# A decode step's attention: TensorE's middle steps as a loop with its own semaphores, and V in loads of 64 KB a partition

## The chip, the cores and the metric

The kernel runs on one core of one Trainium2 chip. The metric is the device time of one execution in microseconds (us): the median of the runs shown is 2523.11 us, the three lie between 2523.05 and 2523.18.

The engines named below are TensorE (PE, matrix products), VectorE (DVE), ScalarE (ACT), GpSimd (POOL) and SyncE (SP), which here issues the loads. They synchronise through semaphores. SBUF is the on-chip memory of 128 partitions, PSUM the accumulators that TensorE writes. HBM, the memory that holds the inputs, is read by 16 DMA engines.

## The reference: what is computed

One token is decoded. A gate mixes an attention over a cache of 65536 positions in 32 heads with a small feed-forward network:

```python
q = (x @ wq).reshape(B, Sq, H, Dh) ...            # H = 32 heads, Dh = 128
scores = jnp.einsum("bhqd,bhkd->bhqk", q, k_cache) * (Dh ** -0.5)   # 65536 keys a head
p = _softmax(scores, axis=-1)
o = jnp.einsum("bhqk,bhkd->bhqd", p, v_cache)
a = o... @ wo                                      # [32*128] @ [4096, 512]
b = (_silu(x @ w_gate) * (x @ w_up)) @ w_down      # 512 -> 1792 -> 512
g = _sigmoid((x * gate_w).sum(-1, keepdims=True))
out = g * a + (1 - g) * b
```

All inputs are bf16. The two caches are 512 MiB each and are read once; everything else together is some 14 MB.

## The kernel before

**Tiles.** A head's 65536 positions are cut into four tiles of 16384 positions; a tile is 128 partitions of 128 positions of 128 elements (4 MiB, 32 KB a partition). There are N = 128 tiles and M = 64 pairs of tiles. A pair's 256 positions of a partition lie one behind the other in HBM, so that a pair is one run of 64 KB a partition. SBUF holds three buffers of 64 KB a partition: two slots for K pairs, taken in turn (`take`, `give`), and one buffer for a V pair, `V_buf`.

**Scores.** VectorE multiplies a K tile by the query, which is repeated on all partitions (line 261), and adds the halves of each row in place, 128 to 64 to 32 to 16 elements (line 265). TensorE adds the 16 that are left by products with a unit matrix, four columns at a time (line 274, `scores`), and VectorE sums the last four (line 289, `fold`).

**Softmax.** After a head's four tiles VectorE takes the maximum of each partition (line 295); ScalarE spreads it on a diagonal (line 297), TensorE turns it to all partitions (line 299), VectorE takes the maximum of it (line 304), and ScalarE computes the exponentials of all four tiles at once with their sums (line 308). TensorE adds the sums over the partitions (line 316, `total`).

**Values.** For a V tile TensorE does 32 products (line 330, `values`): four columns of exponentials are the weights, 512 elements of V the moving operand. The result for a head, 4 x 512 in PSUM with the wanted parts in a diagonal of blocks, is gathered by VectorE (lines 350 and 361, `head_copy`), turned by TensorE (line 367, `head_turn`) and scaled by ScalarE into the column `oT` (line 397). At the end the 32 columns are multiplied by `wo` (line 406).

**The order of the work** is written out by hand: each engine does its instructions in the order in which the program lists them, and the waits follow from what each instruction reads and writes. The main loop (line 424) is unrolled over the K pairs i; a head is two steps, `first` and the other. The values of the pair i - 2 are done in step i. SyncE issues all large loads from one queue (line 114). In a `first` step the V buffer is reloaded in two halves, each as soon as the 32 products on that half are done (lines 442 and 451); in the other step the buffer gets one load of the pair after both tiles' products (line 453). After that, in either kind of step, follows the load of the K pair two steps on, once the scores of the pair that held the slot are done. Scores read the K slot itself.

```python
            values(2 * i - 4)
            if first:
                load_v(2 * i - 2)
```

The first two heads' steps also hold the queries (line 158), the gate and the feed-forward network, whose weights are loaded into the buffer of V. The last tiles are loaded in smaller pieces into the buffers that come free, with the two parts of `wo`.

Of the kernel before, what the change touches and what calls it, by code (L numbers as in the profile page):

```python
# [11 lines left out]
P = 128  # L12

NB = 128
PAIR = 2 * NB
SLOTS = 2

QUAD = 4  # L20
# [5 lines left out]
V_CUTS = {3: (0, 64, NB), 2: (0, 64, NB), 1: (0, 32, 64, 96, 112, NB - TURNED, NB)}  # L26
EARLY = 16
LATE_CUTS = (EARLY, 24, 28, 30, 32)

GROUPED = 28  # L30


@with_exitstack
def kernel(
# [28 lines left out]
    assert Dh == P and G == 4 and NBH == 512 and H * D <= PAIR * Dh  # L63
    scale = float(Dh) ** -0.5

    consts = ctx.enter_context(tc.tile_pool(name="consts", bufs=1))
    ring = ctx.enter_context(tc.tile_pool(name="ring", bufs=1))
    small = ctx.enter_context(tc.tile_pool(name="small", bufs=2))
    psum_s = ctx.enter_context(tc.tile_pool(name="psum_s", bufs=2, space=bass.MemoryType.PSUM))
    psum_o = ctx.enter_context(tc.tile_pool(name="psum_o", bufs=2, space=bass.MemoryType.PSUM))  # L70
    psum_a = ctx.enter_context(tc.tile_pool(name="psum_a", bufs=1, space=bass.MemoryType.PSUM))
    psum_m = ctx.enter_context(tc.tile_pool(name="psum_m", bufs=2, space=bass.MemoryType.PSUM))

    ctx.enter_context(tc.manual_schedule())


    free = list(range(SLOTS))
    held = {}

    def take(name):  # L80
        slot = free.pop(0)
        held[name] = slot
        return ring.tile(
            [P, PAIR * Dh], bf16, name=name.split(".")[0], tag=f"slot{slot}"
        )

    def give(name):
        free.append(held.pop(name))


# [3 lines left out]
    consts.tile([P, 96], bf16, name="fill")  # L94
    xT = consts.tile([P, KT], bf16, name="xT")
    gwT = consts.tile([P, KT], bf16, name="gwT")
    with nc.allow_non_contiguous_dma(reason="small"):
        nc.scalar.dma_start(out=xT, in_=A_x[0, 0, :].rearrange("(p t) -> p t", t=KT))
        nc.scalar.dma_start(out=gwT, in_=gate_w.rearrange("(p t) -> p t", t=KT))

    nc.sync.dma_start(  # L101
        out=V_buf[:, : KT * H * Dh], in_=A_wq.rearrange("(p t) f -> p (t f)", t=KT)
    )
    wq_sb = V_buf[:, : KT * H * Dh].rearrange("p (t f) -> p t f", t=KT)

    K_tiles, V_tiles, S_tiles, F_tiles, P_tiles, O_tiles, q_tiles = {}, {}, {}, {}, {}, {}, {}


    def load(view, cache, m, cuts, start=0):
        h, g = divmod(m, MH)  # L110
        rows = cache[0, h, g * PAIR * P : (g + 1) * PAIR * P, :]
        src = rows.rearrange("(p j) d -> p j d", j=PAIR)
        for a, b in zip(cuts[:-1], cuts[1:]):
            nc.sync.dma_start(out=view[:, a:b, :], in_=src[:, start + a : start + b, :])

    def load_k(m):
        view = take(f"K_t.{m}").rearrange("p (j d) -> p j d", d=Dh)
        load(view, A_k_cache, m, (0, NB, PAIR) if m in (0, M - 1) else (0, PAIR))
        for i in range(2):
            K_tiles[2 * m + i] = view[:, i * NB : (i + 1) * NB, :]  # L120

    def load_v(n, half=0, spare=None):
        if n % G == 0 and spare is None:
            view = V_buf.rearrange("p (j d) -> p j d", d=Dh)
            V_tiles[n], V_tiles[n + 1] = view[:, :NB, :], view[:, NB:, :]
            load(view, A_v_cache, n // 2, (0, PAIR))
        else:
            view = V_buf if spare is None else spare
            view = view[:, half * NB * Dh : (half + 1) * NB * Dh]
            V_tiles[n] = view = view.rearrange("p (j d) -> p j d", d=Dh)  # L130
            load(view, A_v_cache, n // 2, V_CUTS.get(N - n, (0, NB)), n % 2 * NB)

    load_k(0)
    load_k(1)

    ident_f = consts.tile([P, P], f32, name="ident_f")
    make_identity(nc, ident_f[:])
    ident_b = consts.tile([P, P], bf16, name="ident_b")
    nc.scalar.activation(out=ident_b, in_=ident_f, func=ACT.Copy)
    ones_f = consts.tile([P, P], f32, name="ones_f")  # L140
    nc.vector.memset(ones_f, 1.0)

    ones_b = consts.tile([P, P], bf16, name="ones_b")
    nc.vector.memset(ones_b, 1.0)

    qT = consts.tile([P, H], f32, name="qT")
    rowsum = consts.tile([P, H], f32, name="rowsum")
    oT = consts.tile([P, H], bf16, name="oT")
    gval = consts.tile([P, 1], f32, name="gval")
    rg = consts.tile([P, H], f32, name="rg")  # L150
    HD = D // 2
    a_ps = [psum_a.tile([1, HD], f32, name=f"a{i}_ps") for i in range(2)]

    def queries():
        q_ps = psum_m.tile([P, H], f32, name="q_ps", tag="misc")
        for h in range(H):
            for t in range(KT):
                nc.tensor.matmul(
                    q_ps[:, h : h + 1],
                    lhsT=wq_sb[:, t, h * Dh : (h + 1) * Dh],  # L160
                    rhs=xT[:, t : t + 1],
# [398 lines left out]
```

## Time and profile before

| | |
|---|---|
| median of the runs shown | 2523.11 us |
| the profiled execution, its own time | 2523.22 us |
| its span, first to last instruction | 2521.4 us |
| TensorE busy / weight loads | 1274.2 us (51%) / 490.8 us |
| VectorE busy | 2260.4 us (90%) |
| ScalarE busy | 100.5 us (4%) |
| moved by DMA | 1088.42 MB, mean 432 GB/s |
| TensorE's mean granted clock | 0.731 of full speed |

The span is cut into 40 slices, and the rows of digits give the busy tenths of each slice for an engine or for the 16 DMA engines together. The chain goes back from the last instruction, at each step to what released it. In the timeline a row holds the start, the duration, the engine, the line of the kernel and the operation with its operands; instructions that follow one another are merged (x64), and the brackets give the idle time just before and what ended it. SPq rows are issues of loads by SyncE, not the transfers themselves.

### The profile page before, as it was taken

The page shows a single profiled execution, that of the slowest core. Times are in us where ns is not written, and L with a number is a line of the kernel's source. Part 1 is how long each engine was busy: PE and PEld are TensorE (multiplying, and loading weights), DVE is VectorE, ACT ScalarE, POOL GpSimd, SP SyncE. Part 2 cuts the span into 40 slices and gives each one's busy share as a digit, 9 for nine tenths or more (in the row PEclk, how much of TensorE's full clock was granted, in tenths as well). Part 3 has the DMA queues.
Part 4 walks back from the last instruction along what each step waited for, and adds up shares of the span by engine and source line. Part 5 has one row for each costly group of instructions (what it writes and reads, how often), then busy time and mean ns, then how long its engine had stood idle before and what let it go on. Part 6 is the DMA issues. An engine that isn't in the chain of part 4 may idle for free.

```text
span 2521.4 us, 12044 instructions
## 1 busy us (share of the span) xinstructions
PE 1274.2 (51%) x5232; PEld 490.8 (19%) x5232; DVE 2260.4 (90%) x830; ACT 100.5 (4%) x317; POOL 0.7 (0%) x6
## 2 busy tenths in 40 slices
PE   3544654536535455444455453554545544446548
PEld 2211211212212122111122121221211211112213
DVE  5899999989999989899999898999998989999993
ACT  0000000000000000000000000000000000000000
POOL 0000000000000000000000000000000000000000
PEclk8767767767767677676777776776767767677779
DMA  9999999999999999999999999999999999999998
GB/s 415 436 434 433 436 435 430 436 434 433 433 430 436 435 432 432 435 433 442 432 433 432 430 435 434 437 432 433 432 436 432 435 437 429 437 432 432 433 432 374
DMA packets 26888, 1088.42 MB, mean 432 GB/s; under 512 B 3154, under 2 KB 3667, under 8 KB 4947
## 3 DMA queue, kind: packets, MB, share of 16 engines
q1 hardware_dynamic: 26546, 1087.65, 99.8%
q8 instruction: 41, 0.67, 0.1%
q14 instruction: 13, 0.10, 0.0%
q10 hardware_dynamic: 288, 0.00, 0.0%
HBM read 1087.64 MB, written 0.00 MB: 431 GB/s over the span
## 4 chain that ended last, share of the span: by engine, by line
DMA 51%; DVE 46%; PE 2%; issue 1%; another core or an unknown queue 0%; DVEq 0%; SPq 0%; ACT 0%
DMA K_t<-in_A_k_cache_dram 49%; DVE K_t L261 23%; DVE K_t L265 20%; PE S_ps L274 2%; DVE o_row L361 1%; DMA V_buf<-in_A_v_cache_dram 1%; DVE S_sb L289 1%; DVE O_sb L350 1%; DMA wo_late<-in_A_wo_dram 1%; PE O_ps L330 0%; DVE top L304 0%; PE a_ps L406 0%; DVEq L261 0%; SPq L101 0%
## 5 line engine op out<-in xcount | busy, mean ns | idle before, releaser
L261 DVE TENSOR_TENSOR K_t<-K_t,q_sb 128x16384 bf16<-128x16384 bf16 x128 | 1111.7, 8685 | 142.8 <-DMA K_t<-in_A_k_cache_dram 142.8
L330 PE MATMUL O_ps<-V_buf,P_sb 128*4 128x512 bf16 x4032 | 986.4, 409 | 361.4 <-DMA V_buf<-in_A_v_cache_dram 360.5
L265 DVE TENSOR_TENSOR K_t<-K_t 128x2048 bf16<-128x2048 bf16 (+1 forms) x372 | 996.0, 2677 | 8.3
L274 PE MATMUL S_ps<-K_t,ident_b 128*128 128x512 bf16 x576 | 208.3, 503 | 807.2 <-DVE K_t L265 806.8
L330 PEld LDWEIGHTS <-P_sb 128*4 128x4 bf16 x4094 | 364.9, 90 | 980.3 <-issue 534.3
L274 PEld LDWEIGHTS <-ident_b 128*128 128x128 bf16 x576 | 62.4, 113 | 899.4 <-issue 877.3
L289 DVE TENSOR_REDUCE S_sb<-S_ps 128x128 f32<-128x512 f32 x128 | 87.4, 683 | 65.9 <-PE S_ps L274 65.9
L397 ACT ACTIVATE oT<-oh_ps,rg 32x1 bf16<-32x1 f32 x112 | 28.6, 255 | 696.9 <-PE oh_ps L367 695.9
L299 PE MATMUL mT_ps<-diag,ones_f 128*128 128x128 f32 x64 | 24.8, 490 | 60.2 <-ACT diag L297 60.1
L173 ACT ACTIVATE q_sb<-qb_ps 128x128 bf16<-128x128 f32 x32 | 8.9, 278 | 911.6 <-PE qb_ps L171 911.6
L299 PEld LDWEIGHTS mT_ps<-diag,ones_f 128*128 128x128 f32 x64 | 15.6, 303 | 88.4 <-ACT diag L297 88.4
L361 DVE TENSOR_REDUCE o_row<-O_sb 4x128 f32<-4x512 f32 x31 | 31.6, 1020 | 1.1
L297 ACT ACTIVATE diag<-ident_f,m 128x128 f32<-128x128 f32 x32 | 12.8, 401 | 353.9 <-DVE m L295 353.9
L527 DVE CAST out_sb<-a_ps 1x256 bf16<-1x256 f32 x1 | 0.4, 412 | 27.2 <-PE a_ps L406 27.2
L308 ACT ACTIVATE P_sb<-S_sb,bias 128x512 bf16<-128x512 f32 x32 | 23.1, 722 | 1.0
L316 PEld LDWEIGHTS tot_ps<-rowsum,ones_f 128*128 128x128 f32 x64 | 20.7, 324 | 12.1 <-issue 9.2
L295 DVE TENSOR_REDUCE m<-S_sb 128x1 f32<-128x512 f32 x32 | 22.0, 686 | 1.1
L350 DVE TENSOR_TENSOR O_sb<-O_ps,ident_f 4x512 f32<-4x512 f32 x31 | 20.8, 671 | 1.5 <-PE O_ps L330 1.5
L306 ACT ACTIVATE bias<-top 128x1 f32<-128x1 f32 x32 | 6.5, 203 | 298.4 <-DVE top L304 298.4
L316 PE MATMUL tot_ps<-rowsum,ones_f 128*128 128x1 f32 x64 | 13.2, 276 | 0.0
L169 ACT ACTIVATE q_diag<-ident_f,qT 128x128 bf16<-128x128 f32 x32 | 12.8, 400 | 0.4
L321 DVE RECIPROCAL recip<-tot_ps 128x1 f32<-128x1 f32 x32 | 5.1, 161 | 7.8 <-PE tot_ps L316 7.8
(53 smaller groups left out, 115.5 us busy)
## 6 DMA issues: line engine op xcount, KB each, us to landing
V_buf<-in_A_v_cache_dram SPq DMA_DIRECT2D x62, 4096.0 KB, 22.5
K_t<-in_A_k_cache_dram SPq DMA_DIRECT2D x4, 4096.0 KB, 31.8
V_buf<-in_A_v_cache_dram SPq DMA_DIRECT2D x4, 2048.0 KB, 21.9
V_buf<-in_A_wq_dram SPq DMA_DIRECT2D x1, 4096.0 KB, 12.4
wo_early<-in_A_v_cache_dram SPq DMA_DIRECT2D x1, 4096.0 KB, 37.0
wo_late<-in_A_v_cache_dram SPq DMA_DIRECT2D x3, 1024.0 KB, 24.1
wo_early<-in_A_wo_dram SPq DMA_DIRECT2D x1, 2048.0 KB
V_buf<-in_B_w_gate_dram SPq DMA_DIRECT2D x1, 1792.0 KB, 54.6
```

The lines of the kernel that those rows point to most:

```text
L261: yield nc.vector.tensor_tensor(out=K, in0=K, in1=q_rep, op=ALU.mult)
L265: yield nc.vector.tensor_tensor(out=K[:, :, 0:half], in0=K[:, :, 0:half], in1=K[:, :, half : 2 * half], op=ALU.add,)
L274: nc.tensor.matmul(S, lhsT=ident_b, rhs=K_tiles[n][:, :, c : c + QUAD], start=(c == 0), stop=(c == width - QUAD),)
L289: nc.vector.tensor_reduce(out=S_tiles[h][:, g * NB : (g + 1) * NB], in_=F_tiles.pop(n), axis=AXIS.X, op=ALU.add)
L295: nc.vector.tensor_reduce(out=m, in_=S_tiles[h], axis=AXIS.X, op=ALU.max)
L299: nc.tensor.matmul(mT_ps, lhsT=ones_f, rhs=diag, start=True, stop=True)
L308: nc.scalar.activation(out=P_tiles[h], in_=S_tiles[h], func=ACT.Exp, bias=bias, scale=scale, accum_out=rowsum[:, h : h + 1],)
L316: nc.tensor.matmul(tot_ps, lhsT=ones_f, rhs=rowsum[:, h : h + 1], start=True, stop=True)
L330: nc.tensor.matmul(O_tiles[h], lhsT=P_tiles[h][:, g * NB + j : g * NB + j + 4], rhs=V_tiles[n][:, j : j + 4, :], start=(g == 0 and j == 0) ...
L350: nc.vector.tensor_tensor(out=O_sb.rearrange("q (c d) -> q c d", c=4), in0=O.rearrange("q (c d) -> q c d", c=4), in1=diag, op=ALU.mult,)
L361: nc.vector.tensor_reduce(out=dst, in_=src, axis=AXIS.X, op=ALU.add)
L397: nc.scalar.activation(out=oT[part * A : (part + 1) * A, g * QUAD + j : g * QUAD + j + 1], in_=oh_ps[j * A : (j + 1) * A, :], func=ACT.Cop ...
```

## The change

The kernel is written anew inside one section in which every wait and every event is explicit; semaphores belong to the kernel and are cleared at its end by GpSimd. The arithmetic on the tiles is the same, in these pieces:

- TensorE's steps 2 to 62 are one loop of 61 rounds with a fixed body (`tensor_step`). Since a count can't grow in a loop's fixed body, TensorE waits for credits: another engine adds one, `take` waits for one and subtracts it.
- Every V pair ahead of the last step is one load of 64 KB a partition (`load_pair`), issued by SyncE when both tiles of the pair before are done (`load_v`); the K load two steps on follows it. GpSimd waits for the V loads and passes each on as a credit (`tell_of_v`).
- All steps have the same order on TensorE: scores of the first tile, a spread of the query, a total, 64 value products, scores of the second tile, a turn of the output, a turn of the maximum.
- VectorE's last add of a tile writes to a small tile of its own, `T_sb`, which the scores read.
- Exponentials, total and output are made per pair, not per head. The output leaves PSUM by ScalarE (`o_copy`), is turned by four products, and the two halves of a head are added by ScalarE (`add_half_o`).
- The last tiles' loads and those of `wo` have a semaphore for each piece.

```diff
-        if i >= 2:
-            values(2 * i - 4)
-            if first:
-                load_v(2 * i - 2)
...
-            values(2 * i - 3)
-            if first:
-                load_v(2 * i - 1, 1)
-            else:
-                load_v(2 * i - 2)
...
+    def load_v(i):
+        wait(sync, pe_V, 2 * i)
+        load_pair(V_buf, A_v_cache, i, v_in)
+
+    def sync_step(m):
+        load_v(m - 1)
+        if m + 2 < M:
+            wait(sync, pe_S, 2 * m + 2)
+            load_k(m + 2)
...
+    def tell_of_v(i):
+        wait(pool, v_in, 16 * (i + 1))
+        pool.sem_inc(c_V, 1)
...
+    def vector_step(m):
+        h, b = divmod(m, MH)
+        width, to = (WIDTH, T_sb) if m < M - 1 else (LAST, None)
+        last = product(2 * m)
+        if b == 0:
+            top_of(h - 1)
+        else:
+            fold(2 * m - 1)
+        add_halves(2 * m, width, last, to)
+        last = product(2 * m + 1)
+        fold(2 * m)
+        if b == 1:
+            weight(h - 1, m - 1)
+        add_halves(2 * m + 1, width, last, to)
+        if b == 1:
+            row_max(h, fold(2 * m + 1))
...
+    def scalar_step(m):
+        h, b = divmod(m, MH)
+        if b == 0:
+            head_bias(h - 1)
+        wait(act, pe_V, 2 * (m - 2))
+        exponentials(h - 1, b, P_sb, PAIR).then_inc(c_P, 1)
+        if m == M - 1:
+            return
+        if b == 1:
+            query(h + 1, True)
+        else:
+            act.sem_inc(c_q, 1)
+        wait(act, pe_V, 2 * (m - 2) + 2)
+        o_copy(h - 1).then_inc(c_o, 1)
+        wait(act, pe_o, m - 1)
+        if b == 0:
+            marks["half_o"] = ac(copy(half_o[:, 0:1], oh))
+            act.sem_inc(c_m, 1)
+        else:
+            ac(head_out(h - 1, add_half_o()))
+            head_diag(h, True)
...
+    def take(credit):
+        pe.wait_ge(credit, 1)
+        pe.sem_inc(credit, -1)
...
+    def tensor_step():
+        take(c_S[0])
+        scores(0, T_sb, WIDTH)
+        take(c_q)
+        query_spread()
+        take(c_P)
+        total()
+        take(c_V)
+        for i in range(2):
+            pe_V(values(P_sb[:, i * NB : (i + 1) * NB], V_half[i], 0, NB, i == 0, i == 1))
+        take(c_S[1])
+        scores(1, T_sb, WIDTH)
+        take(c_o)
+        head_turn()
+        take(c_m)
+        max_turn()
...
+    with tc.tile_critical():
+        prologue()
+        for m in range(2, M):
+            vector_step(m)
+            scalar_step(m)
+            if m < M - 1:
+                sync_step(m)
+            tell_of_v(m - 2)
+        sync_end()
...
+        with pe.Fori(0, M - 3):
+            tensor_step()
+        tensor_end()
+        for engine in (pe, act, dve):
+            engine.sem_inc(done.sem, 1)
+
+        pool.wait_ge(done.sem, 3)
+        pool.wait_ge(out_in.sem, 16)
+        pool.sem_clear(range(first_sem.num, last_sem.num + 1))
```

## The prediction

> **What bounds the kernel now.** I read the page's slices and queues first, then the chain that ended last, then one head's timeline (TensorE, VectorE and SyncE separately), then the waits of SyncE.
>
> ```profile
> DMA  9999999999999999999999999999999999999998
> DMA packets 26888, 1088.42 MB, mean 432 GB/s; under 512 B 3154, under 2 KB 3667, under 8 KB 4947
> q1 hardware_dynamic: 26546, 1087.65, 99.8%
> q8 instruction: 41, 0.67, 0.1%
> ...
> DMA 51%; DVE 46%; PE 2%; issue 1%; another core or an unknown queue 0%; DVEq 0%; SPq 0%; ACT 0%
> ```
>
> The reader is to see that the 16 DMA engines never rest: queue 1 alone fills 99.8% of their span. VectorE is 90% busy and takes nearly half of the chain, but it waits for K in every step, so it follows the DMA. The timeline of one step (K pair to K pair) shows it:
>
> ```profile
> 1236.67 0.33 SPq L114 DMA_DIRECT2D V_buf<-in_A_v_cache_dram  x1
> 1245.62 0.33 SPq L114 DMA_DIRECT2D K_t<-in_A_k_cache_dram  x1
> ...
> 1247.91 8.69 DVE L261 TENSOR_TENSOR K_t<-K_t,q_sb 128x16384 bf16<-128x16384 bf16 x1 [0.87 <-DMA K_t<-in_A_k_cache_dram]
> ...
> 1264.77 1.86 PE L274 MATMUL S_ps<-K_t,ident_b 128*128 128x512 bf16 x4 [16.45 <-DVE K_t L265]
> ...
> 1266.44 0.42 PE L316 MATMUL tot_ps<-rowsum,ones_f 128*128 128x1 f32 x2
> ...
> 1267.16 14.77 PE L330 MATMUL O_ps<-V_buf,P_sb 128*4 128x512 bf16 x64 [0.30 <-DMA V_buf<-in_A_v_cache_dram]
> ...
> 1275.06 7.23 SPq L114 DMA_DIRECT2D V_buf<-in_A_v_cache_dram  x2
> ...
> 1284.59 0.33 SPq L114 DMA_DIRECT2D K_t<-in_A_k_cache_dram  x1
> ...
> 1286.42 8.69 DVE L261 TENSOR_TENSOR K_t<-K_t,q_sb 128x16384 bf16<-128x16384 bf16 x1 [2.67 <-DMA K_t<-in_A_k_cache_dram]
> ```
>
> K lands at 1247.9, the V pair 19.25 us later at 1267.1, the next K at 1286.4. A step is 38.51 us, in which 16 MiB arrive: 435.7 GB/s. The V pair issued at 1236.67 had 11.2 us of K ahead of it in the queue; the next V, in two halves, is issued at 1275.06 and 1281.96 (the row's end less 0.33), again 11.3 us ahead of the landing at 1286.4. That lead is what keeps the queue full, and the change touches it.
>
> I then took all 59 intervals between K landings (starts of the first product of a step that waited for a K load) from 123.93 to 2410.52, 2286.59 us in all, and split them by what V was loaded in them. The 30 with two half loads have a median of 38.745 us, the 29 with one pair load 38.53 us. Two intervals of either kind are some 1.3 us longer, cause unseen.
>
> **The change part by part**, against the profiled execution's own 2523.22 us (span 2521.4, 1.8 around it; the median of the timed runs is 2523.11, so 0.1 less). A measurement here can tell about 0.2%, 5.0 us, from no change.
>
> *The V loads.* 30 pairs of 4 MiB loads become 30 loads of 8 MiB. By the two medians a step with one load is 0.215 us shorter: 30 x 0.215 = 6.4 us off. Ends: nothing, if the difference between the two kinds of step has another cause, and 13.3 us, if every interval came down to 38.53 (2286.59 - 59 x 38.53). I take 6.4, the row of the very operation.
>
> *When the V buffer is refilled.* Before, in every second step, half of it is reloaded after 32 matmuls. Now SyncE waits for all 64 (the V event counts) before any of it, in every step, and the lead falls from 11 us to what is left after 64 matmuls. Queued behind that wait on SyncE is the K load two steps on; behind the K load waits VectorE. The loop is: V landed, the relay through GpSimd, 64 matmuls, issue, landing. The 64 matmuls at one go (29 groups in the middle of the trace) take 14.63 to 15.96 us, mean 15.23; the first few run at a granted clock of 0.5. From their end to the issue it is 0.03 us (the second half above: 1281.93 to 1281.96). From issue to landing on an empty queue the nearest row is the 4096 KB load of the query weights, 12.4 us, where 4 MiB take 9.63 at the rate of the steps: 2.77 us over the bytes, so 19.27 + 2.77 = 22.04 for a pair. The lower end is the output's store, which is issued at 2519.35 while the span ends at 2521.4: at most 2.05 over the bytes, 21.3. Sum: 15.23 + 0.03 + 22.04 = 37.30, against 38.53 for the DMA: 1.23 us to spare, before the relay.
>
> The relay and what else stands ahead of the matmuls: GpSimd's wait and its increment (its queue holds nothing else in these steps), TensorE's wait and decrement (the nearest row is a semaphore hop of 0.06 from ScalarE's diagonal to its matmul), and in program order the scores of the first tile (they start 16.86 us after K landed, 2.4 ahead of V; a step that begins with a fold, 0.68, instead of the maximum, 0.28, starts them 0.4 later), one spread of the query (0.23) and the total (0.42). I put the delay at 0.3 to 1.5 us, part of it at half clock, where a delayed matmul is made up for later; 0.7 as a middle. That leaves 0.5 us a step: the forecast is that V is refilled in time, at no cost. The other end is 15.96 + 1.5 + 22.07 - 38.53 = 1.0 us a step, 61 us over 61 looped steps. Less than nothing it can't be, as the bytes set 38.53.
>
> The Trainium skill (DMA: Bandwidth & Descriptors, Anatomy of one DMA) fits a load as about 2.0 us plus the bytes at 436 GB/s, on GpSimd's path; by it a pair would take 21.2 us instead of 22.04, the spare would be 2.0, and the sum the same. No run shown has an 8 MiB load on an empty queue.
>
> *VectorE.* It loses the two operations that took a head's output out of PSUM (0.67 + 1.02 a head) and gains a sum of two columns (about 0.16, as the other small ones). Its adds now each follow an explicit wait; an event instruction on SyncE has a median of 28 ns, so some 14 of them are 0.4 a step. All of this is hidden: VectorE waits 2.67 and 0.87 us for K in the two steps of a head. Late next is K. If that cover were gone, each us would also push the first scores, and with them the V refill.
>
> *TensorE and ScalarE.* Each step now has a spread, a total of two columns, and a head turn by four float32 products (eight rows of line 380 take 1.02), and ScalarE copies the output (0.59, line 344). TensorE has 16.45 us idle before the first scores of a step, ScalarE is 4% busy: nothing. The second tile's scores move behind all 64 matmuls. VectorE finishes that tile 34.5 us after K landed; the matmuls end at about 19.2 + 0.7 + 15.2 = 35.1; scores 1.03, fold 0.69, maximum 0.69 reach 37.6, ahead of the next K at 38.53. If the matmuls end over 0.9 later, VectorE starts late in every second step, but it has 1.8 a step on average to make that up.
>
> *TensorE's program* is a loop of 61 rounds. Its instruction fetch, 0.67 MB in 41 packets on the same engines, is 1.5 us at 434 GB/s. Ends: 1.5 off and the price in rival 2; I take 1.0 off.
>
> *The start.* The first V reload was issued in halves at 114.50 and 121.41; now it goes at 121.4 whole, landing at 143.4, with the K of 122.75 behind it landing at 162.7, against 162.6 before. Ends 0 and 2.8 (an emptied queue); I take 0.5.
>
> *The end.* GpSimd waits for three engines and the store and clears about 50 semaphores. Nearest: 28 ns each if single, 1.4; or one instruction in place of the present waits of SyncE at the end (0.7 and 0.6), -0.5. I take 0.7. The last loads each get a semaphore of their own and lose their waits (9.0 and 4.1 us on lines 183 and 185), but the queue is never empty there: nothing.
>
> Sum: 2523.2 - 6.4 - 1.0 + 0.5 + 0.7 = 2517.0 us, 0.24% faster.
>
> **The rivals.**
>
> 1. *The refill is late (the other side).* The loop V landed, 64 matmuls, issue, landing becomes longer than 38.53 us and sets the step. It decides where the time from the V landing to the last value matmul passes 16.5 us (38.53 - 22.04). For it: 29 measured groups reach 15.96 without any relay, and with so small a lead an uneven finish of the 16 engines is no longer averaged out. Against it: the mean leaves 1.2 us. At 0.6 us a step it gives 61 x 0.6 = 37 on top of the other terms: 2517 + 37 = 2554. From 0.2 to 1.0 a step: 2529 to 2578.
>
> 2. *The loop's jump costs.* At the jump back TensorE has to get its program again, two packets of 16 KB a round (0.67 MB / 41) or 2 MB in all: 1.3 MB more than before, +3 us, and if a fetch falls among the value matmuls, every us beyond the 0.5 spare is 61 us. For it: the queue for instructions shares the full engines. Against it: the jump stands in a 16 us idle stretch, and a body of some 190 instructions is small. With 0.5 us lost a step: 2517 + 4 + 31 = 2552. The Trainium skill (Runtime: NRT & Kernel Launch, Instruction fetch mechanics) says that a taken branch to a page outside the current two-page window must fetch it before going on; nothing in the profile before shows a branch.
>
> 3. *The merged load gains nothing.* The 0.215 us belong to something else in that step. For it: the four long intervals show that the DMA's pace has causes I don't see. Against it: 21 of the 29 pair steps and 25 of the 30 half steps lie within 0.1 of their own kind's median. Then 2517.0 + 6.4 = 2523.4, no change.
>
> **How the numbers follow.** The refill in time: 0.45; its own range is 2511 (the gain up to 12) to 2521, of which 0.31 lies below 2518.1, the 0.2% line, and 0.14 above. Rival 1: 0.39, of which 0.06 is so small (up to 0.15 us a step) that it ends within 0.2%. Rival 2: 0.08, slower. Rival 3: 0.08, same. So faster 0.31, same 0.28, slower 0.41. The likeliest case gives 2517.0. The range reaches down to 2511 and, for the late refill, up to 2565: some 0.08 of rivals 1 and 2 lies above and 0.04 below.
>
> **What would show it.** Right: intervals between K landings all at 38.53; groups of 64 value matmuls ending within 16.5 us of the V landing; VectorE's idle time still put down to K; few instruction packets. Wrong: intervals well over 38.6 with the DMA share of the slices below 9 tenths or the rate below 430 GB/s, the chain running through value matmuls and V loads (rival 1); TensorE idle among the matmuls of a step with instruction packets beside it (rival 2); alternating intervals gone but none at 38.53 (rival 3). The time is wrong if the lead of 0.5 us is not there: it is the difference of sums near 38 us, and 2% of either decides it.

## The result, and the profile after

The changed kernel takes 2553.6 us (median of four runs, 2552.57 to 2557.16) against 2523.14 us before: a ratio of 1.0122, 95% interval 1.0104 to 1.0139. It is 1.2% slower. The profiled execution took 2553.62 us, with a span of 2551.8 us.

The page of the changed kernel, its slices, queues and chain:

```profile
DMA  9999999999999999999999999999999999999998
DMA packets 22389, 1087.84 MB, mean 426 GB/s; under 512 B 2657, under 2 KB 3170, under 8 KB 4450
...
q1 hardware_dynamic: 22082, 1087.65, 99.1%
q8 instruction: 5, 0.08, 0.0%
...
PE 2%; DVE 0%; ACT 0%; issue 0%
```

The queue of the loads still looks full: every slice but the last reads 9. But its share fell from 99.8% to 99.1%, and the rate from 432 to 426 GB/s with the same bytes. The slices are too coarse for this loss; the rate shows it. The instruction queue went from 41 packets to 5. The chain of this trace covers only the last 2% of the span and says nothing of the steps.

The landing of each K pair is the start of VectorE's first product in a step that waited for a K load. Cut at these landings, the two spans compare like this:

| stretch | before | after | difference | the prediction had |
|---|---|---|---|---|
| start, up to the landing at 162.64 / 167.76 | 162.6 | 167.8 | +5.1 | +0.5 |
| the next 58 steps | 2247.9 | 2267.1 | +19.2 | -7.4 |
| last K landing (2410.52 / 2434.83) to the end | 110.9 | 117.0 | +6.1 | +0.7 |
| span | 2521.4 | 2551.8 | +30.4 | -6.2 |

A step went from 38.76 us on average to 39.09. The loss isn't spread evenly. These are rows of the timeline of the changed kernel, two steps in a row (SyncE's issues of V, VectorE's first product of each step, the value products; the brackets hold the idle time before and what ended it):

```profile
1067.25 0.33 SPq L174 DMA_DIRECT2D V_buf<-in_A_v_cache_dram  x1
1069.98 8.69 DVE L254 TENSOR_TENSOR K_buf<-K_buf,q_sb 128x16384 bf16<-128x16384 bf16 x1 [4.93 <-DMA K_buf<-in_A_k_cache_dram]
1091.51 16.53 PE L457 MATMUL O_ps<-V_buf,P_sb 128*4 128x512 bf16 x64 [1.88 <-PEq L432]
1108.08 0.33 SPq L174 DMA_DIRECT2D V_buf<-in_A_v_cache_dram  x1
1110.92 8.69 DVE L254 TENSOR_TENSOR K_buf<-K_buf,q_sb 128x16384 bf16<-128x16384 bf16 x1 [0.41 <-DMA K_buf<-in_A_k_cache_dram]
1130.40 15.87 PE L457 MATMUL O_ps<-V_buf,P_sb 128*4 128x512 bf16 x64 [0.22 <-PEq L432]
1146.30 0.33 SPq L174 DMA_DIRECT2D V_buf<-in_A_v_cache_dram  x1
1149.58 8.69 DVE L254 TENSOR_TENSOR K_buf<-K_buf,q_sb 128x16384 bf16<-128x16384 bf16 x1 [4.72 <-DMA K_buf<-in_A_k_cache_dram]
```

The V pair issued at 1067.25, 2.73 us ahead of the K landing at 1069.98, lets its products start 24.26 us after the issue; TensorE stood idle for 1.88 us, and the next K landed 40.94 us after the last one. The V pair issued at 1108.08 had much the same lead, 2.84 us, and was on time: products after 22.32 us, a step of 38.66 us.

I call the time from the issue of a V pair to the next K landing its lead. All 56 steps of the changed kernel that the trace shows whole, with the undisturbed steps of this kernel, 38.63 us, as the measure:

| lead of the V load | steps | products start over 20.0 us behind the K landing | mean step, us |
|---|---|---|---|
| 2.4 to 3.1 us | 14 | 6 | 39.63 |
| 3.1 to 3.75 | 22 | 4 | 38.99 |
| 3.75 to 4.25 | 11 | 2 | 38.93 |
| over 4.25 | 9 | 0 | 38.67 |

On time means a start 19.5 us behind the K landing. The 12 late steps hold 19.2 us of the 25.6 us by which these steps exceed 38.63 us each. A late V load makes the K pair behind it late by about as much.

What is late in such a step is a small part of the load. The trace records the landing of each load in sixteen parts, as many as there are DMA engines. Of the V load issued at 1067.25, fourteen parts are in 21.55 to 22.19 us after the issue, the last two after 23.98 and 24.08 us; of the one issued at 1108.08 all sixteen are in after 21.39 to 22.14 us. In each of the 12 late steps the last one to three parts are over 1 us behind the eighth. In the kernel before, the parts of a K load lie even further apart, 4.6 us from first to last (median) and up to 7.5, against 1.5 and 3.5 here, and no step is late: with the longer lead an engine that is ahead has the next load in its queue.

The packets, the pieces in which the DMA engines move a load, show the loss as well. Summed over the 7 us behind each of 58 V issues, a DMA engine of the changed kernel (mean of the sixteen) stands idle for 7.5 us and loses 13.5 us in packets of 64 KB that take longer than their usual 2.42 us. That is 21 us, about the 19.2 us that the steps lost. In the kernel before neither shows: none of its packets of 64 KB in these steps takes over 3 us, 155 of the changed kernel's do.

SyncE's waits in the changed kernel (engine and line, what was waited for: us in total, times, longest) show who holds that load back:

```profile
SPq L174 <- PE O_ps L457: 2291.4, 61, 39.8
SPq L174 <- PE S_ps L436: 97.9, 61, 39.6
```

SyncE waits for the value products in every step; the K load's own condition, the scores behind them, adds about 1 us (97.9 less the one wait of 39.6, over the other 60).

### The profile page after: what moved, and what is told of

Its sections match the earlier page's. It is cut to its first block, busy times and chain, and to the rows that moved or that the text cites. A ratio compares the mean times of both kernels' runs of the same rounds, so it can differ in the third digit from the quotient of the medians.

```text
span 2551.8 us, 13959 instructions
## 1 busy us (share of the span) xinstructions
PE 1344.4 (53%) x5813; PEld 559.9 (22%) x5813; DVE 2217.6 (87%) x802; ACT 187.6 (7%) x503; POOL 0.7 (0%) x6
## 3 DMA queue, kind: packets, MB, share of 16 engines
q1 hardware_dynamic: 22082, 1087.65, 99.1%
## 5 line engine op out<-in xcount | busy, mean ns | idle before, releaser
L254 DVE TENSOR_TENSOR K_buf<-K_buf,q_sb 128x16384 bf16<-128x16384 bf16 x128 | 1112.1, 8688 | 204.3 <-DMA K_buf<-in_A_k_cache_dram 204.3
L265 DVE TENSOR_TENSOR K_buf<-K_buf 128x8192 bf16<-128x8192 bf16 x252 | 849.4, 3371 | 4.3
L436 PE MATMUL S_ps<-T_sb,ident_b 128*128 128x512 bf16 x488 | 180.1, 505 | 1026.4 <-PEq L432 1026.2
L457 PEld LDWEIGHTS O_ps<-V_buf,P_sb 128*4 128x4 bf16 x3968 | 352.6, 90 | 621.7 <-issue 184.6
L436 PEld LDWEIGHTS S_ps<-T_sb,ident_b 128*128 128x128 bf16 x488 | 44.9, 110 | 1115.3 <-issue 1099.0
L323 ACT ACTIVATE O_sb<-O_ps 4x512 f32<-4x512 f32 x63 | 63.5, 1008 | 1306.3 <-PE O_ps L457 1306.3
L265 DVE TENSOR_TENSOR T_sb<-K_buf 128x2048 bf16<-128x2048 bf16 x122 | 149.4, 1224 | 4.2
L465 PE MATMUL oh_ps<-ident_f,O_sb 4*128 4x1 f32 x504 | 64.6, 245 | 10.2 <-PEq L432 9.4
L465 PEld LDWEIGHTS oh_ps<-ident_f,O_sb 4*128 4x128 f32 x504 | 60.7, 186 | 40.0 <-issue 39.5
L453 PEld LDWEIGHTS tot_ps<-rs,ones_f 128*128 128x128 f32 x126 | 34.2, 330 | 18.0 <-issue 17.9
```

Of the source, the lines that this page charges most:

```text
L254: return dv(dve.tensor_tensor(out=K, in0=K, in1=q_rep, op=ALU.mult))
L265: ins = dve.tensor_tensor(out=to, in0=K[:, :, 0:half], in1=K[:, :, half : 2 * half], op=ALU.add)
L323: return act.activation(out=out, in_=in_, func=ACT.Copy, scale=scale)
L436: ins = pe.matmul(S_ps[n % 2], lhsT=ident_b, rhs=src[:, :, c : c + QUAD], start=(c == 0), stop=(c == width - QUAD),)
L453: pe_t(pe.matmul(tot[:, :n], lhsT=ones_f, rhs=rs[:, :n], start=True, stop=True))
L457: ins = pe.matmul(O_ps, lhsT=probs[:, j : j + 4], rhs=view[:, j : j + 4, :], start=(opens and j == start), stop=(closes and j == stop - 4),)
```

## The experiments

The theory to be tested, A: one load of a whole pair can be issued only after all 64 products, some 3.6 us ahead of the K landing instead of 10 to 12, and that is too late. Against it stood: the loop or its jump, the size of the load, and TensorE's half clock in the first products.

### The old kernel with single loads

The kernel before, with every V pair as one load after both tiles' products:

```diff
-            if first:
-                load_v(2 * i - 2)
...
-            if first:
-                load_v(2 * i - 1, 1)
-            else:
-                load_v(2 * i - 2)
+            load_v(2 * i - 2, pair=True)
```

> The kernel before, with one part of the change alone: every V pair is one load of 8 MiB, issued after both tiles' value products; its order on TensorE, its waits and its unrolled program stay. Theory A (the refill comes too late: V landed, 64 products, issue, landing is as long as a step): slower than 2523, since in the steps that are not the first of a head the first tile's scores stand between the two tiles' products, so the issue comes some 1 to 4 us before the next K lands, where it was 11 us; 2545 to 2590. Theory B (the loop, its credits and its relay cost the time, the loads do not): 2517, the 6 us that one load saves over two in 30 steps. Theory C (an 8 MiB V load is itself slower or less even than two of 4 MiB): some 2540, with no relation to the lead.

Measured: 2584.87 us (2569.67 to 2590.97), ratio 1.0252 [1.0234, 1.0269]. In the profiled execution, the fastest of the five, a step takes 39.44 us on average. This part of the change alone, with no loop and no new semaphores, makes the old kernel 2.5% slower. (It is slower than the changed kernel, but it also isn't its order: in every second step the first tile's scores stand between the two tiles' products.) The forecast that V is refilled in time at no cost falls here already.

### The changed kernel with V in halves

```diff
-        wait(sync, pe_V, 2 * i)
-        load_pair(V_buf, A_v_cache, i, v_in)
+        for t in range(2):
+            wait(sync, pe_V, 2 * i - 1 + t)
+            load_tile(V_half[t], A_v_cache, 2 * i + t, v_in)
...
-        wait(pool, v_in, 16 * (i + 1))
+        wait(pool, v_in, 16 * (i + 1) if i == 0 else 32 * i + 16)
```

> The changed kernel, one part undone and more: in every step V is loaded in two halves, each issued when its own tile's 32 products are done; loop, credits and relay stay (the relay waits for both halves). Theory A: the first half is issued some 10 us before the next K lands, the late steps go; steps of 38.75 us (two half loads a step, by the median of such steps before), 61 x (39.09 - 38.75) = 21 us off and some 8 more at the start and the end: 2523 to 2532. Theory B: no change, 2550 to 2557. Theory C: as A.

Measured: 2530.14 us, ratio 1.0026 [1.0016, 1.0036]: 23.5 of the 30.5 us are back. The timeline of one step:

```profile
1235.40 7.24 SPq L178 DMA_DIRECT2D V_buf<-in_A_v_cache_dram  x2
1246.72 8.69 DVE L255 TENSOR_TENSOR K_buf<-K_buf,q_sb 128x16384 bf16<-128x16384 bf16 x1 [1.22 <-DMA K_buf<-in_A_k_cache_dram]
1266.23 15.82 PE L458 MATMUL O_ps<-V_buf,P_sb 128*4 128x512 bf16 x64 [0.25 <-PEq L433]
```

The first half goes out at 1235.40, 11.3 us ahead of the landing; the products start 19.51 us behind it, and take 15.82 us, no less than in the changed kernel. Steps average 38.74 us. The start is back as well: the K pair that landed at 201.17 before lands at 201.38. What remains is the end, 119.1 us from the last K landing (2409.67) to the span's end at 2528.8, against 110.9: TensorE is told only when both halves are there, where the kernel before began on the first half alone. (The next experiment takes 5.0 us of it off.)

### A credit for each half

The same, with a semaphore and a credit for each half:

```diff
+            load_tile(V_half[t], A_v_cache, 2 * i + t, (v_in, vb_in)[t])
...
         pool.sem_inc(c_V, 1)
+        if i:
+            wait(pool, vb_in, 16 * (i))
+        pool.sem_inc(c_V, 1)
...
-        take(c_V)
         for i in range(2):
+            take(c_V)
```

> As the run with V in halves in every step, and TensorE gets a credit for each half and starts on the first as soon as it has landed. Theory A: steps stay at 38.68 (nothing is late any more); at the end, where a chain of TensorE's work runs from the landing of the last pair of V in the looped steps to the last product, that chain starts up to 9 us earlier: 6 to 8 us off 2530, so 2522 to 2524. If the end's loss has another cause: 2530.

Measured: 2524.48 us (2524.11 to 2526.06), ratio 1.0006 [0.9997, 1.0015]. Steps of 38.74 us, 114.1 us behind the last K landing. With V cut in halves and passed on in halves, the loop and the new semaphores are worth the same as the old kernel, as far as can be measured: the loss lies in how V is loaded and passed on.

### The loop written out

```diff
-        with pe.Fori(0, M - 3):
+        for _ in range(M - 3):
             tensor_step()
```

> The changed kernel with TensorE's 61 rounds written out one after the other in place of the loop; credits, order and loads the same. Theory A: no change, 2550 to 2557; the instruction packets return to some 40. Theory B in its form that the jump back costs: 2517 to 2530. Theory C: no change.

Measured: 2563.0 us (2558.75 to 2569.72), ratio 1.0163 [1.0144, 1.0183]. The queues of this kernel's page:

```profile
q8 instruction: 47, 0.77, 0.1%
```

Written out, the kernel is some 9 us slower than with the loop, not equal or faster. Its late steps are as many (12 of 57); its other 45 steps average 38.97 us where those of the loop average 38.77, which by itself is 9 us (the spans of the two profiled executions differ by 7.0 us). So the jump costs nothing that shows, and the rival of the jump falls. That the instruction loads are the reason fits the trace: each of the 42 further packets is 16 KB and takes a DMA engine some 0.9 us, and the 40 steps into which such a packet falls average 39.34 us, the 18 others 38.88 us. No run moved these packets alone.

### More products, a later load

The first value product is done eight more times in each step, 1.75 us at 13.98/64 us a product:

```diff
+        for _ in range(8):
+            pe.matmul(O_ps, lhsT=P_sb[:, 0:4], rhs=V_half[0][:, 0:4, :], start=True, stop=True)
         for i in range(2):
             pe_V(values(...))
```

> The changed kernel with the step's first value product done eight times more ahead of itself (each overwrites, the result is the same): 8 x 0.216 = 1.73 us more from the landing of V to its refill. Theory A: the lead falls by 1 to 1.7 us, and as most steps are already late each gets longer by 0.9 to 1.7 us: 55 to 105 us, 2605 to 2660. Theory C: under 10 us, as TensorE has 16 us idle a step.

Measured: 2648.45 us, ratio 1.051 [1.0489, 1.0531]; the span grew by 86.9 us, 1.42 us in each of 61 steps. In its trace the 72 products take 17.61 us on average, where the 64 took 15.61, so 2.0 us were added, and seven tenths of it reach the end. TensorE is about half idle in the changed kernel (53% busy), and yet most of what is put ahead of the V issue lengthens the step. The circle V landed, products, issue, landing sets the step.

### Half-size loads, but late

Two loads of 4 MiB, both after all 64 products; the GpSimd relay waits for both:

```diff
-        load_pair(V_buf, A_v_cache, i, v_in)
+        if i == 0:
+            load_pair(V_buf, A_v_cache, i, v_in)
+            return
+        for t in range(2):
+            load_tile(V_half[t], A_v_cache, 2 * i + t, (v_in, vb_in)[t])
```

> The changed kernel with each V pair asked for as two loads of 4 MiB, both only after all 64 value products (so as late as the one load was), and TensorE told when both have landed. Theory A (the refill is asked for too late: what counts is how long before the K pair has landed the next V load is issued): nothing is gained by the smaller loads alone, 2548 to 2565 us, and the mean distance between K landings stays at 39.0 us or more. Theory C (the size of the load itself is at fault, two loads of half the size run better): 2525 to 2535 us, 38.7 us a step, as when the halves were also asked for early.

Measured: 2576.51 us (2571.68 to 2583.92), ratio 1.0219 [1.0203, 1.0235]; steps of 39.39 us.

```profile
1233.62 0.83 SPq L180 DMA_DIRECT2D V_buf<-in_A_v_cache_dram  x2
1238.30 8.69 DVE L262 TENSOR_TENSOR K_buf<-K_buf,q_sb 128x16384 bf16<-128x16384 bf16 x1 [5.47 <-DMA K_buf<-in_A_k_cache_dram]
1273.77 0.81 SPq L180 DMA_DIRECT2D V_buf<-in_A_v_cache_dram  x2
1277.03 8.69 DVE L262 TENSOR_TENSOR K_buf<-K_buf,q_sb 128x16384 bf16<-128x16384 bf16 x1 [0.81 <-DMA K_buf<-in_A_k_cache_dram]
```

The same two loads that gave 38.74 us a step when the first went out 11 us ahead give 39.39 us when the first goes out as late as here, 4.7 and 3.3 us ahead in the two steps shown. It isn't the size of the load; it is when it is issued. That it is 23 us worse than one load, issued as late, was not expected; the first load's lead is the same (3.57 us on average against 3.60), and the second follows 0.48 us later. Why the extra load costs 0.3 us a step stays open.

### A warm TensorE

Two tries at a larger lead by shorter products: 24 idle products ahead of the first scores, so that the value products don't begin at half clock.

```diff
+        take(c_w)
+        for _ in range(24):
+            idle_product()
         take(c_S[0])
```

The credit `c_w` comes from VectorE, in the first try as a plain increment:

> The changed kernel with 24 idle products of the value products' form ahead of each step's first scores, started by a credit from VectorE after the step's first product of K; they write where the step's first value product writes afterwards, so nothing of the result changes. They should leave TensorE at the full granted clock when V lands. Theory A: the 64 products fall from 15.6 to some 14.1 us, the lead of the V issue over the landing of K grows from 3.7 to about 5.2 us, and most of the 0.55 us a step over 38.53 goes: 2525 to 2537. Theory B: no change or a few us more, 2553 to 2560. Theory C: no change, 2553.

Measured: 2553.08 us, ratio 1.0127 [1.011, 1.0143]. The increment ran ahead of VectorE's product: the idle products stood at 1220.94, right behind the K landing at 1220.58, and the value products still took 15.5 us on average. In the second try the increment comes after the product is done:

> As the run with the idle products, but the credit for them is given when the step's first product of K is complete, not when it is issued, so that they run in the 8 us before the first scores and not 12 us earlier. They write where the step's first value product writes afterwards. Theory A, with the need read from the steps of the changed kernel (a V issue at least 4.4 us ahead of the landing of K: steps of 38.63 us; 3.5 ahead: 38.9; 3.0 ahead: 39.4): the 64 products take 14.0 to 14.3 us in place of 15.6, the lead goes from 3.7 to about 5.1, steps go to 38.65: (39.09 - 38.65) x 61 = 27 us off, 2522 to 2532. Theory C (the 8 MiB loads are uneven whatever the lead): 2550 to 2556.

Measured: 2551.68 us (2542.71 to 2554.88), ratio 1.01 [1.0084, 1.0115]. This missed. The value products came down to 15.0 us on average (13.97 at the least, and close to it in only 23 of 58 steps), and the lead rose from 3.60 to 4.27 us. But 16 of 57 steps were late, no fewer than before. Steps with a lead over 4.25 us were fine (2 of 27 late, 38.76 us on average), those below were late more often than in the changed kernel (14 of 30). Together with the changed kernel, its written-out form and the last experiment below: below 4.25 us of lead 52 of 158 steps were late, above it 2 of 68; with the first try counted as well, 62 of 199 and 4 of 82. Within 2.5 to 4.25 us the lead only sets how likely lateness is. In a single step it is the last few of the sixteen parts that come late; why these, and why in that step, stays open.

### Every second pair in halves

```diff
+        if i and i % 2 == 0:
+            wait(sync, pe_V, 2 * i)
+            load_pair(V_buf, A_v_cache, i, v_in)
+            return
+        for t in range(2):
+            wait(sync, pe_V, 2 * i - 1 + t)
+            load_tile(V_half[t], A_v_cache, 2 * i + t, (v_in, vb_in)[t])
```

> As the run before it, but only every second V pair is loaded in halves, the others in one load, which is the order of the kernel before under the loop and the credits. Theory A: the halves let the first tile's products run early, so the one load of the next step is issued some 10 us ahead and nothing is late. If a load in halves costs what the steps of the kernel before say (0.2 us), half of the steps are shorter than 38.68 by 0.1 to 0.2: 3 to 6 us less than the run before it, 2516 to 2521, which is below the kernel before. If the halves cost nothing: the same as the run before it.

Measured: 2542.8 us, ratio 1.0076 [1.0063, 1.009], between all halves (2524.48) and all single loads (2553.6). Missed, for a plain reason: the loop's body takes the scores' credit ahead of the values. A half that lands 9.6 us behind K isn't used before the scores are through, at 17.5 us or so, and the single load after it goes out as late as in the changed kernel (1249.93 against a landing at 1254.28). The kernel before takes the first half's products ahead of the scores in every second step, and that is what lets its single loads go out early.

### The loop over heads

So the loop's body becomes a head, two steps with different orders; in the second the first half's products stand ahead of the scores (30 rounds, and one step written out). V is loaded as in the experiment above, and in the last step, too, 32 products run ahead of the scores:

```diff
+    def tensor_step(b):
+        if b:
+            take(c_P)
+            total()
+            take(c_V)
+            pe_V(values_half(0))
+        take(c_S[0])
+        scores(0, T_sb, WIDTH)
...
-        with pe.Fori(0, M - 3):
-            tensor_step()
+        with pe.Fori(0, (M - 4) // 2):
+            tensor_step(0)
+            tensor_step(1)
+        tensor_step(0)
```

> The changed kernel with TensorE's loop over heads (30 rounds of two steps, and one step written out): pairs of odd number come as two loads, each issued as soon as its half of the products is done; pairs of even number come as one load; in every second step the first half's products stand ahead of the scores, so that they run when that half has landed (about 9.6 us after the K pair) and the one load after them is issued some 11 us before the next K pair has landed. Theory A (lead decides, the loop saves the instruction loads): 38.5 to 38.6 us in the steps behind a single load and 38.7 in the others, 38.65 on average, and 2514 to 2521 us, under the kernel before. If the loop's own order costs (rival: the credits' chain, a longer body), 2523 us or more.

Measured: 2527.16 us (2526.55 to 2527.98), ratio 1.0015 [1.0006, 1.0024].

```profile
1217.29 9.14 PE L466 MATMUL O_ps<-V_buf,P_sb 128*4 128x512 bf16 x32 [10.04 <-PEq L441]
1227.44 7.07 PE L466 MATMUL O_ps<-V_buf,P_sb 128*4 128x512 bf16 x32
1234.54 0.33 SPq L175 DMA_DIRECT2D V_buf<-in_A_v_cache_dram  x1
1246.11 8.69 DVE L263 TENSOR_TENSOR K_buf<-K_buf,q_sb 128x16384 bf16<-128x16384 bf16 x1 [0.41 <-DMA K_buf<-in_A_k_cache_dram]
...
2408.43 8.69 DVE L263 TENSOR_TENSOR K_buf<-K_buf,q_sb 128x16384 bf16<-128x16384 bf16 x1 [0.43 <-DMA K_buf<-in_A_k_cache_dram]
...
2475.99 3.59 PE L445 MATMUL S_ps<-K_buf,ident_b 128*128 128x512 bf16 x8 [4.36 <-DVE K_buf L274]
```

The single load goes out 11.6 us ahead as expected, and though it is one load of 8 MiB, none of its 64 KB packets takes over 3 us. Four of 58 steps are still 0.9 us longer than the others, and two of them start their products over 20 us behind the K landing; an 8 KB packet of a second instruction queue (q14) falls into each of the four, but into eight ordinary steps as well. The last K landing is 2.1 us earlier than before (2408.43 against 2410.52). The time was missed in two places: a step takes 38.72 us on average instead of 38.65, 4 us in all, and the end, 116.4 us behind that landing, is 5.5 us longer than before: TensorE is idle 4.36 us, and the eight scores of the last tile take 3.59 us.

With the scores of tile N-2 first again, and 56 products ahead of the last scores:

```diff
+        scores_direct(N - 2, LAST)
         take(c_P)
...
-        values(lower, V_half[1], 0, NB // 2, False, False)
+        values(lower, V_half[1], 0, 3 * NB // 4, False, False)
         scores_direct(N - 1, LAST)
-        values(lower, V_half[1], NB // 2, 3 * NB // 4, False, False)
```

> The head loop with the last step's order changed: the scores of tile N-2 stand ahead of the value products again, and 56 of the last pair's 64 products (48 in the kernel before) run before the scores of tile N-1, so that TensorE isn't idle ahead of them (4.36 us in the head loop, 1.75 us in the kernel before). The stretch behind the last K pair's landing was 116.4 us in the head loop and 110.9 us in the kernel before; if TensorE's idle time and the cold clock behind it made the difference, it comes to 109 to 112 us and the time to 2519 to 2522.5 us. If it was the loads, it stays near 2526 us.

```profile
2461.99 13.08 PE L466 MATMUL O_ps<-V_buf,P_sb 128*4 128x512 bf16 x56
2475.00 1.90 PE L445 MATMUL S_ps<-K_buf,ident_b 128*128 128x512 bf16 x8
2478.84 0.49 PE L459 MATMUL qm_ps<-diag,ones_f 128*128 128x128 f32 x2 [1.94 <-ACT diag L332]
```

Measured: 2524.59 us (2523.08 to 2525.03), ratio 1.0003 [0.9994, 1.0012]; 113.2 us behind the last K landing, a little more than expected. The idle time ahead of the scores and the slow scores are gone, but 1.94 us of idle time now stand ahead of the turn of the maximum. That is 3.2 of the 5.5 us by which the end was too long, so the cause named was a part of it, not all. No form of the loop that I ran is measurably faster than the kernel before.

### The end alone

The changed kernel with only the loop's last V pair in halves:

```diff
+        if i < M - 3:
+            wait(sync, pe_V, 2 * i)
+            load_pair(V_buf, A_v_cache, i, v_in)
+            return
+        for t in range(2):
+            wait(sync, pe_V, 2 * i - 1 + t)
+            load_tile(V_half[t], A_v_cache, 2 * i + t, (v_in, vb_in)[t])
```

> The changed kernel with one load split: the last V pair of the loop comes as two loads of 4 MiB, the first issued after its half of the products before, and TensorE's last step takes the halves one by one. The loop's steps stay as they are. Theory A (the tail's 6 us come from that pair landing whole): the stretch behind the last K landing comes from 117.0 us to 110 to 112 us, and the time to 2546 to 2549.5 us; if that pair has nothing to do with it, 2552 to 2556 us.

First the end of the kernel before (its last K landing, its value products and its last scores), then that of the changed kernel, then this one's:

```profile
2410.52 8.69 DVE L261 TENSOR_TENSOR K_t<-K_t,q_sb 128x16384 bf16<-128x16384 bf16 x1 [1.10 <-DMA K_t<-in_A_k_cache_dram]
...
2463.25 10.62 PE L330 MATMUL O_ps<-V_buf,P_sb 128*4 128x512 bf16 x48
2475.61 1.89 PE L274 MATMUL S_ps<-K_t,ident_b 128*128 128x512 bf16 x8 [1.75 <-DVE K_t L265]
```

```profile
2493.51 11.83 PE L457 MATMUL O_ps<-V_buf,P_sb 128*4 128x512 bf16 x48 [5.02 <-PEq L432]
2505.27 1.90 PE L436 MATMUL S_ps<-K_buf,ident_b 128*128 128x512 bf16 x8
```

```profile
2438.08 8.69 DVE L264 TENSOR_TENSOR K_buf<-K_buf,q_sb 128x16384 bf16<-128x16384 bf16 x1 [1.52 <-DMA K_buf<-in_A_k_cache_dram]
...
2491.67 10.95 PE L467 MATMUL O_ps<-V_buf,P_sb 128*4 128x512 bf16 x48
2504.25 1.90 PE L446 MATMUL S_ps<-K_buf,ident_b 128*128 128x512 bf16 x8 [1.63 <-DVE K_buf L275]
```

Measured: 2549.74 us (2546.95 to 2552.59), ratio 1.01 [1.0085, 1.0116]. In the changed kernel TensorE waits 5.02 us for the whole pair, and the last scores stand behind its products, 70.4 us behind the last K landing (2434.83). With the halves it waits for VectorE instead, as in the kernel before: 66.2 us against 65.1 there. The end shrinks from 117.0 to 112.7 us, 4.3 of its 6.1 us, somewhat less than expected. In this kernel and in all with the loop VectorE makes a third add (1.22 us) also in tiles N-4 and N-3, whose scores the kernel before took at 32 columns.

## Why the prediction was wrong, point by point

**What bounds the kernel.** Right: the queue of the loads, and in it the lead of the V loads, "what the change touches".

**The refill: the step that failed.** The prediction added 15.23 + 0.03 + 22.04 + 0.7 and found 0.5 us to spare in 38.53. Its parts:

- The products: 15.61 us on average instead of 15.23 (14.35 to 16.87), 0.4 more.
- End to issue: 0.03, right.
- The relay: products started 19.5 us behind K in on-time steps, 19.25 in the step read before; 0.2 to 0.3 us, less than the 0.7 taken.
- From issue to landing: 22.04, from one row, the load of the query weights. That is the term that was wrong. With a lead under 3.1 us the last part of a V load lands 22.0 to 22.3 us behind the issue in on-time steps, 23.2 to 24.4 in late ones. The prediction's own row gave the lower end of that, and a spare of half a us was set against a quantity that spreads over more than two. Its first rival named the reason, an uneven finish of the 16 engines that a small lead no longer averages out; the sum gave it no price.

The lead that these terms give was right (38.53 - 19.25 - 0.3 - 15.23 = 3.7 us; measured 3.6). But the number that decides wasn't "16.5 us from landing to last product": most steps kept below that, 0.3 + 15.6 on average, and one in five came late all the same. The lower and upper ends of the refill were given as 0 and 1.0 us a step; by the table above it cost 0.33 us a step against the kernel before. The value was taken at the lower end where the spare was a small difference of large terms.

The Trainium skill (DMA: Bandwidth & Descriptors, Anatomy of one DMA) fits a load on GpSimd's path as about 2.0 us, taken as constant, plus the bytes; an estimate by it is 21.2 us for a pair. These traces of loads issued by SyncE differ: 22.0 us at the least, and up to 24.4 in late steps. A reader who goes by the constant finds even more to spare.

**The merged load** was to give 6.4 us, from a median of 38.53 us behind single loads against 38.745 behind halves. That term is nothing. Two steps in a row have a median of 77.31 us in the kernel before, 77.31 in the loop over heads, and 77.36 in the changed kernel with all halves. The two kinds of step of the kernel before sum to the same: what one gained the next one gave back. The changed kernel's single loads reach steps of 38.60 us at best, not 38.53. The pace of the bytes is half of the two steps, 38.65 us, where the prediction took 38.53. The third rival was right on this.

**TensorE's program**: the 1.0 us taken can't be told from the noise; the steps of the loop with halves are together 0.8 us shorter than those of the kernel before, which it could account for. Where loads go out late it is worth 9 us. The rival that the jump costs was wrong in sign: the Trainium skill (Runtime: NRT & Kernel Launch, Instruction fetch mechanics) says that a taken branch to a page outside the window stalls, and that kernels are better unrolled. Here the loop of 61 rounds took 5 instruction packets, and written out it took 47 and was slower by 9 us.

**The start** was +5.1 instead of +0.5. The prediction moved the first V reload from 114.50 to 121.4. These rows of the changed kernel show it at 126.31:

```profile
110.98 15.29 PE L457 MATMUL O_ps<-V_buf,P_sb 128*4 128x512 bf16 x64
126.31 0.33 SPq L174 DMA_DIRECT2D V_buf<-in_A_v_cache_dram  x1
148.62 15.25 PE L457 MATMUL O_ps<-V_buf,P_sb 128*4 128x512 bf16 x64 [3.32 <-PEq L432]
167.76 8.69 DVE L254 TENSOR_TENSOR K_buf<-K_buf,q_sb 128x16384 bf16<-128x16384 bf16 x1 [1.42 <-DMA K_buf<-in_A_k_cache_dram]
```

The products begin at 110.98, behind the scores, and take 15.29 us; the prediction took over the times of the products before. The load then runs its 22.3 us to the next products, and K lands 41.5 us behind the issue. With halves the start is that of the kernel before.

**The end** was +6.1 instead of +0.7. "The queue is never empty there: nothing" looked at the queue and not at TensorE, which there does set the end: from the last scores on it works almost without a pause for 43 us. What the prediction passed over is that the loop's last V pair now lands whole, so that TensorE starts on it later (2493.51 - 2434.83 = 58.7 us behind the last K landing, against 2463.25 - 2410.52 = 52.7). The experiment on the end gave 4.3 us of it back.

**The rival.** The first one, a late refill, is what happened, and its time of 2554 meets the 2553.6 measured. That it is so close is chance: it had 37 us for the refill in the steps and 6.4 + 1.0 off for other parts; the runs show 19 in the steps, 11 at the two ends, and nothing off for the merging.

## What to carry to other kernels

In a kernel that is bound by its loads, the time at which each load is issued, as us ahead of the landing of the load in front of it, is to be read before any saving in the number of loads. With a lead not much above what a load takes beyond its bytes (2.77 us by the prediction's row) the queue was not safe here: 3.6 us of lead made one load in five late, and with 10 to 12 us at most two steps of 58 were late; splitting a load in two so that its first half can go out early was worth 1.1%, and merging two loads was worth nothing. When a spare of half a us is the difference of sums near 38, the forecast should not take it as zero cost; it should ask how far each term spreads.

## What the runs showed of the hardware

- A load of 8 MiB issued 2.5 to 3.1 us ahead of the last landing took 22.0 to 24.4 us from the issue to its last part, in steps that look alike (24.08 and 22.14 us for the two loads of the first timeline above). Twelve of its sixteen parts were in after 21.5 to 22.4 us in all of them. Which load it hits stays open.
- The sixteen parts of a load land unevenly, over 4.6 us (median) for the K loads of the kernel before. With 10 to 12 us of lead that cost nothing that shows; with 3.6 us the engines lost 21 us behind 58 V issues, idle or in longer packets.
- A loop on TensorE took 42 instruction packets of 16 KB fewer than its rounds written out. Where loads go out late it was 0.2 us a step faster in steps that were otherwise undisturbed. With early loads the same saving doesn't show.
- Eight score products in the last steps took 1.9 us when TensorE had been idle for 1.63 to 1.75 us, and 3.3 to 3.6 us behind idle times of 2.4 us and more (1.90 behind 1.63, 1.89 behind 1.75 and 3.59 behind 4.36 in the rows of the ends above; 3.33 behind 2.40 with a credit for each half). The granted clock was 1.00 in the first two, and 0.50 from 2474.3 to 2481.0 in the loop over heads and from 2476.6 to 2479.9 with a credit for each half. A clock lost that way at the end is time on the path.
